# A pointwise product with 12 KB input runs, 3 KB output runs and a ring of one-supertile slots

## The chip, the cores and the metric

The kernel runs on one core of a Trainium2 chip. The metric is the device time of one execution in microseconds, the median of several runs; lower is better. Engine names are those of the profile: PE multiplies matrices, PEld is its weight load, DVE and ACT work on vectors, POOL and SP here mostly issue DMAs.

## The reference

```
out = xp[:, :H, :W, :] * dw[0, 0]          # k = 1: no padding, one product per channel
return jnp.einsum('bhwc,cd->bhwd', out, pw)
```

x is (1, 384, 384, 384), dw is (1, 1, 384) and pw is (384, 384), all bf16. So it is 147,456 rows of 384 channels, each channel scaled by dw, times a 384 x 384 matrix. Both kernels scale pw by dw once (w_r) and then compute x times w_r.

## The kernel before

**Rows and tiles.** 512 rows are a supertile, 288 in all. A chunk is one to four supertiles: 1, 1, 2, 4 at the start, then 68 chunks of four, and 4, 2, 2 at the end, 75 chunks. A chunk of x is loaded into one of four buffers X (line 143). Within each supertile, partition p gets four neighbouring rows, 3 KB in one run.

**Transposes.** PE contracts over the partitions, so channels have to lie there. DVE transposes 32 x 32 blocks of 32-bit words, a word being two neighbouring channels (line 248). There are twelve instructions for a chunk, each for one block of 64 channels and every other slot, all supertiles of the chunk at once; each writes runs of 32 neighbouring words. Their output goes to one of two buffers T, each for a whole chunk.

**Product.** For a supertile PE makes 48 matmuls (line 170): 6 channel blocks x 2 channels of a word (par) x 4 partition groups q of 32. The four groups work side by side, each into a PSUM buffer of its own; two sets of four are used in turn (PS). The set is free when ACT (s_a) and DVE (s_d) have copied it. PE's program is straight-line for the first four chunks and the last three, and between them a loop of 34 turns with eight supertiles each. PE waits for T once per chunk (lines 189 and 208).

**Copies and stores.** ACT copies q = 0, 1 and 2 of a supertile in three instructions (line 295), DVE copies q = 3 (line 289), to one of three output buffers O. DVE's program is in order: in front of each copy stand a share of the next chunk's transposes. When the chunk's last supertile is copied, POOL issues four stores (line 307), each from 32 partitions, with runs of 768 B in the output.

**Order of the queues.** SP issues all loads of x, one after the other, each as soon as the transposes of the chunk four before it are done; in front of the third it waits for pw. POOL issues all stores. At the start ACT issues dw and two loads of pw, SP the other two. dw is spread over all partitions, masked and reduced on DVE (lines 257 to 269) to give each partition its scalars (dwsel); DVE then makes the twelve pieces of w_r (line 226). The first supertile's matmuls each wait for their piece only (first_ever).

Of the kernel before, what the change touches and what calls it, by code (L numbers as in the profile page):

```python
# [10 lines left out]
ADD = mybir.AluOpType.add  # L11
MUL = mybir.AluOpType.mult

GMAX = 4
PRO = [1, 1, 2, 4]


def _plan(n_groups: int):
    if n_groups < 24:
        chunks = []  # L20
        left = n_groups
        for g in PRO:
            if left <= 0:
                break
            g = min(g, left)
            chunks.append(g)
            left -= g
        while left > 0:
            g = min(GMAX, left)
            chunks.append(g)  # L30
            left -= g
        return chunks, 0, []
    L = (n_groups - 16) // 8
    E = n_groups - 8 - 8 * L
    epi = []
    rest = E - 4
    while rest >= GMAX:
        epi.append(GMAX)
        rest -= GMAX
    if rest > 0:  # L40
        epi.append(rest)
    epi += [2, 2]
    assert sum(PRO) + 8 * L + sum(epi) == n_groups
    return list(PRO), L, epi


@with_exitstack
def kernel(
# [6 lines left out]
    NX: int = 4,  # L55
    NO: int = 3,
    pw_on_sp: int = 1,
):
    nc = tc.nc
# [5 lines left out]
    assert C == 384 and D == 384 and N % 512 == 0  # L65
    NB = C // 64
    m_max = 4 * GMAX
# [3 lines left out]

    pro, L, epi = _plan(N // 512)
    chunks = pro + [GMAX] * (2 * L) + epi
    NT = len(chunks)
    n_pro = len(pro)
    t_loop0, t_loop1 = n_pro, n_pro + 2 * L
    row0 = [0] * NT
    j0 = [0] * NT
    acc_r = acc_j = 0
    for t, g in enumerate(chunks):  # L80
        row0[t], j0[t] = acc_r, acc_j
        acc_r += 512 * g
        acc_j += g
    NST = acc_j
    if L:
        assert j0[t_loop0] % 8 == 0 and t_loop0 % 2 == 0
# [7 lines left out]
    dwb = consts.tile([P, C], BF16, name="dwb")  # L94
    ones = consts.tile([P, 4, 32], F32, name="ones")
    maskq = consts.tile([P, 4, 32], F32, name="maskq")
    mask32 = consts.tile([P, 32], F32, name="mask32")
    prod = consts.tile([P, NB * 2, 32], F32, name="prod")
    dwsel = consts.tile([P, NB * 2], F32, name="dwsel")
    warm = consts.tile([P, 1], F32, name="warm")  # L100

    Xs = [bufp.tile([P, m_max, C], BF16, name=f"X{i}") for i in range(NX)]
    Ts = [bufp.tile([P, NB, m_max, 64], BF16, name=f"T{i}") for i in range(2)]
    Os = [bufp.tile([P, m_max, D], BF16, name=f"O{i}") for i in range(NO)]
    PS = [[psum.tile([P, D], F32, name=f"ps{s}_{q}") for q in range(4)] for s in range(2)]

    s_x = [nc.alloc_semaphore(f"s_x{i}") for i in range(NX)]
    s_t = [nc.alloc_semaphore(f"s_t{i}") for i in range(2)]
    s_pe = nc.alloc_semaphore("s_pe")
    s_a = [nc.alloc_semaphore(f"s_a{i}") for i in range(8)]  # L110
    s_d = [nc.alloc_semaphore(f"s_d{i}") for i in range(8)]
# [3 lines left out]
    s_pw_sw = nc.alloc_semaphore("s_pw_sw")  # L115
    s_mask = nc.alloc_semaphore("s_mask")
    s_wr = nc.alloc_semaphore("s_wr")
    s_dv = nc.alloc_semaphore("s_dv")

    with tc.tile_critical():  # L120
        dw_row = dw.rearrange("a e c -> (a e) c")
        pw_v = pw.rearrange("(b w r) d -> w b (r d)", w=32, r=2)

        def load_pw(eng, q):
            sem = s_pw_sw if eng is nc.gpsimd else s_pw
            eng.dma_start(pw_r[32 * q : 32 * q + 32].rearrange("w b r d -> w b (r d)"), pw_v).then_inc(sem, 16)
# [4 lines left out]
        if not pw_on_sp:  # L131
            load_pw(nc.scalar, 0)
            load_pw(nc.scalar, 1)
        for t in range(NT):
            if t == 1 and pw_on_sp:
                load_pw(nc.sync, 0)
                load_pw(nc.sync, 1)
# [5 lines left out]
            d = nc.sync.dma_start(Xs[i][:, : 4 * G, :].rearrange("p (g sl) c -> p g (sl c)", sl=4), src)  # L143
            if t >= NX:
                tp = t - NX
                d._wait_ge(s_t[tp % 2], tp // 2 + 1)
            d.then_inc(s_x[i], 16)

        nc.gpsimd.memset(ones[:], 1.0).then_inc(s_mask)
        nc.gpsimd.affine_select(  # L150
            out=maskq[:],
            in_=ones[:],
            pattern=[[-32, 4], [-1, 32]],
            compare_op=mybir.AluOpType.is_equal,
            fill=0.0,
            base=0,
            channel_multiplier=1,
        )._wait_ge(s_mask, 1).then_inc(s_mask)

        nc.scalar.copy(warm[:], ones[:, 0, 0:1])._wait_ge(s_mask, 1)  # L160

        def pe_supertile(tb, g, j, wait_a=None, wait_d=None, first_ever=False):
            s = j % 2 if isinstance(j, int) else None
            for b in range(NB):
                for par in range(2):
                    for q in range(4):
                        lhsT = Ts[tb][32 * q : 32 * q + 32, b, 4 * g : 4 * g + 4, :].rearrange("p s e -> p (s e)")[
                            :, par::2
                        ]
                        mm = nc.tensor.matmul(  # L170
                            PS[s][q][:],
                            lhsT=lhsT,
                            rhs=w_r[32 * q : 32 * q + 32, b, par, :],
                            start=(b == 0 and par == 0),
                            stop=(b == NB - 1 and par == 1),
                            tile_position=(32 * q, 0),
                        )
                        if b == 0 and par == 0 and q == 0 and wait_a is not None:
                            mm._wait_ge(*wait_a)
                        elif b == 0 and par == 0 and q == 3 and wait_d is not None:  # L180
                            mm._wait_ge(*wait_d)
                        elif first_ever and q == 0:
                            mm._wait_ge(s_wr, 2 * b + par + 1)
                        if b == NB - 1 and par == 1 and q == 3:
                            mm.then_inc(s_pe)

        def pe_chunk_static(t):
            tb = t % 2
            nc.tensor.wait_ge(s_t[tb], t // 2 + 1)
            for g in range(chunks[t]):  # L190
                j = j0[t] + g
                wa = wd = None
                if j >= 2:
                    wa = (s_a[(j - 2) % 8], (j - 2) // 8 + 1)
                    wd = (s_d[(j - 2) % 8], (j - 2) // 8 + 1)
# [150 lines left out]
```

## Time and profile before

| what | value |
|---|---|
| time, median of 3 runs (lowest to highest) | 613.34 us (612.08 to 613.62) |
| profiled execution, span | 610.8 us |
| PE, PEld, DVE, ACT, POOL busy | 572.1, 422.0, 452.0, 359.4, 193.1 us |
| moved by DMA in the span, mean rate | 228.12 MB, 373 GB/s |
| queue of stores (POOL): packets, MB | 32512, 113.27 |
| queue of SP's loads: packets, MB | 38480, 113.84 |

The profile is of one execution; no time other than its span was taken of that execution itself, so its span is set beside the median of the runs, 2.5 us above it. Busy times are unions: four matmuls side by side count once. Rows of a chain or a timeline begin with start and duration in us; in the groups by line, "busy, mean ns of one" is followed by the idle time in front of them and by what ended it. "issue" means that the engine waited for nothing that the profile shows. The granted clock is a share of PE's full clock.

### The profile page before, as it was taken

To read this page: it belongs to the slowest core of one execution; us is meant where nothing else is said; L and a number is where in the kernel's file an instruction comes from. 1 tells how busy PE (TensorE), PEld (TensorE's weight loads), DVE (VectorE), ACT (ScalarE), POOL (GpSimd) and SP (SyncE) were. 2 spreads that over 40 slices of the span, in tenths; PEclk is the share of its full clock that TensorE was granted. 3 is DMA by queue.
4 is the path that set the end of the run, shared out by engine and by line. 5 is a ranking of instruction groups with operands and counts; after the bars stand their busy time and mean duration, and the time that the engine had idled before them with its cause. 6 is when DMAs were issued, how large, how long until landed. Compare 5 with 4: busy or idle time off the path is not lost.

```text
span 610.8 us, 30631 instructions
## 1 busy us (share of the span) xinstructions
PE 572.1 (94%) x13824; PEld 422.0 (69%) x13824; DVE 452.0 (74%) x1203; ACT 359.4 (59%) x866; POOL 193.1 (32%) x306
## 2 busy tenths in 40 slices
PE   1979999999999998999989999999998999999991
PEld 0546888888888665888866777766666666777771
DVE  4866778877777866877767787777875777878860
ACT  0445666666666664666655666666665556666661
POOL 0422333333333232333322333333332233333333
PEclk9999999999999998999999999999999999999997
DMA  6999999999999999999999999999999999999976
GB/s 171 407 405 385 348 382 390 397 397 387 390 381 383 396 387 379 387 398 387 383 391 401 391 396 373 384 385 393 394 393 391 383 394 386 392 396 399 359 215 182
DMA packets 71584, 228.12 MB, mean 373 GB/s; under 512 B 6081, under 2 KB 11585, under 8 KB 71553
## 3 DMA queue, kind: packets, MB, share of 16 engines
q0 software_dynamic: 32512, 113.27, 51.0%
q1 hardware_dynamic: 38480, 113.84, 48.5%
q10 hardware_dynamic: 560, 0.69, 0.5%
q8 instruction: 9, 0.15, 0.1%
q14 instruction: 23, 0.18, 0.1%
HBM read 114.52 MB, written 113.25 MB: 373 GB/s over the span
## 4 chain that ended last, share of the span: by engine, by line
PE 69%; DMA 24%; DVE 3%; issue 1%; POOL 1%; ACT 1%; SPq 0%; ACTq 0%; DVEq 0%
PE ps_0_82 L170 25%; PE ps_0_86 L170 24%; DMA X_76<-in_x_dram 11%; DMA X_74<-in_x_dram 9%; PE ps_3_85 L170 5%; PE ps_3_89 L170 5%; PE ps_1_87 L170 4%; PE ps_1_83 L170 4%; DMA out_dram<-O_79 2%; DVE T_78 L248 2%; DMA pw_r<-in_pw_dram 2%; PE ps_2_88 L170 1%; PE ps_2_84 L170 1%; POOL out_dram L307 1%; ACT O_79 L295 0%
## 5 line engine op out<-in xcount | busy, mean ns | idle before, releaser
L170 PE MATMUL ps_0_82<-w_r,T_77 32*128 32x384 bf16 x876 | 157.6, 325 | 12.6 <-DVE w_r L226 12.5
L170 PE MATMUL ps_3_85<-w_r,T_77 32*128 32x384 bf16 x876 | 157.2, 326 | 4.8 <-DVE O_80 L289 2.7
L170 PE MATMUL ps_2_84<-w_r,T_77 32*128 32x384 bf16 x876 | 157.8, 325 | 0.0
L170 PE MATMUL ps_1_83<-w_r,T_77 32*128 32x384 bf16 x876 | 157.8, 325 | 0.0
L170 PE MATMUL ps_3_89<-w_r,T_78 32*128 32x384 bf16 x864 | 153.1, 322 | 1.4 <-issue 1.4
L170 PE MATMUL ps_0_86<-w_r,T_77 32*128 32x384 bf16 x864 | 152.7, 322 | 1.6 <-issue 1.6
L170 PE MATMUL ps_3_85<-w_r,T_78 32*128 32x384 bf16 x852 | 150.0, 321 | 4.3 <-DVE O_79 L289 2.4
L170 PE MATMUL ps_1_87<-w_r,T_78 32*128 32x384 bf16 x864 | 153.1, 322 | 0.1
L170 PE MATMUL ps_0_86<-w_r,T_78 32*128 32x384 bf16 x864 | 153.1, 322 | 0.0
L170 PE MATMUL ps_2_88<-w_r,T_78 32*128 32x384 bf16 x864 | 153.1, 322 | 0.0
L170 PE MATMUL ps_2_88<-w_r,T_77 32*128 32x384 bf16 x864 | 152.7, 322 | 0.0
L170 PE MATMUL ps_1_87<-w_r,T_77 32*128 32x384 bf16 x864 | 152.7, 322 | 0.0
L170 PE MATMUL ps_3_89<-w_r,T_77 32*128 32x384 bf16 x864 | 152.5, 322 | 0.0
L170 PE MATMUL ps_0_82<-w_r,T_78 32*128 32x384 bf16 x852 | 150.5, 321 | 1.5 <-DVE T_78 L248 1.5
L170 PE MATMUL ps_2_84<-w_r,T_78 32*128 32x384 bf16 x852 | 150.7, 321 | 0.0
L170 PE MATMUL ps_1_83<-w_r,T_78 32*128 32x384 bf16 x852 | 150.7, 321 | 0.0
L170 PEld LDWEIGHTS ps_0_82<-w_r,T_77 32*128 32x128 bf16 x876 | 79.8, 94 | 47.0 <-DVE w_r L226 13.3
L307 POOL DMA_DIRECT2D out_dram<-O_79 x100 | 64.4, 650 | 148.9 <-ACT O_79 L295 147.0
L307 POOL DMA_DIRECT2D out_dram<-O_81 x100 | 64.1, 647 | 131.1 <-ACT O_81 L295 128.4
L307 POOL DMA_DIRECT2D out_dram<-O_80 x100 | 63.9, 646 | 128.4 <-ACT O_80 L295 128.4
L170 PEld LDWEIGHTS ps_0_86<-w_r,T_78 32*128 32x128 bf16 x864 | 80.3, 93 | 31.0 <-issue 2.6
L170 PEld LDWEIGHTS ps_0_82<-w_r,T_78 32*128 32x128 bf16 x852 | 77.0, 93 | 35.6 <-issue 9.7
(53 smaller groups left out, 1930.3 us busy)
## 6 DMA issues: line engine op xcount, KB each, us to landing
out_dram<-O_79 POOLq DMA_DIRECT2D x96, 384.0 KB, 9.5
out_dram<-O_80 POOLq DMA_DIRECT2D x92, 384.0 KB, 9.5
out_dram<-O_81 POOLq DMA_DIRECT2D x92, 384.0 KB, 9.5
X_76<-in_x_dram SPq DMA_DIRECT2D x18, 1536.0 KB, 23.6
X_73<-in_x_dram SPq DMA_DIRECT2D x18, 1536.0 KB, 24.1
X_74<-in_x_dram SPq DMA_DIRECT2D x17, 1536.0 KB, 23.9
X_75<-in_x_dram SPq DMA_DIRECT2D x17, 1536.0 KB, 24.7
X_75<-in_x_dram SPq DMA_DIRECT2D x2, 768.0 KB, 10.7
```

What stands on the lines that cost most here:

```text
L170: mm = nc.tensor.matmul(PS[s][q][:], lhsT=lhsT, rhs=w_r[32 * q : 32 * q + 32, b, par, :], start=(b == 0 and par == 0), stop=(b == NB - 1 a ...
L248: ins = nc.vector.transpose(out=Tw[:, b, h:mm_:2, :], in_=Xw[:, h:mm_:2, 32 * b : 32 * b + 32])
L307: sd = nc.gpsimd.dma_start(dstv[sl], Os[o][32 * sl : 32 * sl + 32, : 4 * G, :])
```

## The change

- A chunk is now mapped in one piece: partition p gets 4L neighbouring rows of a chunk of L supertiles (12 KB in one run for L = 4). Supertile j of the chunk takes the rows k L + j of each partition, k = 0 to 3. The output row of group q, PSUM partition m = 4 i + k, is then q 128 L + m L + j, so a store has runs of L rows (3 KB for L = 4) on all 128 partitions.
- To put the rows in that order, a transpose writes its 32 words with a step of four words ("p b (i k) -> p b k i"). There are two transposes for a supertile, each of three channel blocks (384 words per partition), with a semaphore of its own.
- T holds one supertile per slot, two slots. DVE's order is: copy of jj, transposes of jj + 2, which wait for PE's half of jj.
- PE is a loop of 144 turns with two supertiles each. It waits for all twelve w_r before the loop, and for each half of T. s_pe counts half supertiles.
- ACT copies q = 0 to 2 in one instruction; PS is one PSUM tile of four 2 KB rows per set.
- SP issues loads and stores, one store per chunk; there are four buffers O. POOL issues no DMA.
- dw is loaded by 32 partitions in pieces of two channels and copied to the four groups on DVE; w_r is made half by DVE and half by ACT. The loads of x no longer wait for pw.
- Chunks: 1, 1, 2, then 70 of four, then 2, 1, 1.

```diff
-        nc.scalar.dma_start(dwb[:], dw_row.to_broadcast((P, C))).then_inc(s_dw, 16)
...
-            if t == 2:
-                nc.sync.wait_ge(s_pw, 16 * 4)
-            i = t % NX
-            G = chunks[t]
-            src = xf[row0[t] : row0[t] + 512 * G, :].rearrange("(g p sl) c -> p g (sl c)", p=P, sl=4)
...
+        def load_x(t):
+            L = chunks[t]
+            r = 512 * s0[t]
+            src = xf[r : r + 512 * L, :].rearrange("(p s) c -> p (s c)", p=P)
+            d = nc.sync.dma_start(Xs[t % NX][:, : 4 * L, :].rearrange("p s c -> p (s c)"), src)
+            if t >= NX:
+                je = s0[t - NX] + chunks[t - NX] - 1
+                d._wait_ge(s_t[je % 2][1], je // 2 + 1)
+            d.then_inc(s_x[t % NX], 16)
+
+        def store(t):
...
+            nc.sync.wait_ge(s_d[je % 2], je // 2 + 2)
+            dst = of[r : r + 512 * L, :].rearrange("(q p j) d -> p q (j d)", q=4, p=P)
+            d = nc.sync.dma_start(dst, Os[t % NO][:, : 4 * L * D].rearrange("p (q e) -> p q e", q=4))
+            d._wait_ge(s_a[je % 2], je // 2 + 2)
+            d.then_inc(s_o[t % NO], 16)
...
+        nc.scalar.dma_start(dwt[:], dw_v).then_inc(s_dw, 16)
+        load_x(0)
+        load_pw(nc.scalar, 2)
+        load_pw(nc.sync, 0)
+        load_pw(nc.scalar, 3)
+        load_pw(nc.sync, 1)
+        for t in range(1, NX):
+            load_x(t)
         for t in range(NT):
...
+            if t + NX < NT:
+                load_x(t + NX)
+            store(t)
...
+        def supertile(s, rv):
             for b in range(NB):
                 for par in range(2):
                     for q in range(4):
...
+                        if par == 0 and q == 0 and b in (0, 3):
+                            nc.tensor.wait_ge(s_t[s][b // 3], rv)
                         mm = nc.tensor.matmul(
...
+                            lhsT=Ts[s][32 * q : 32 * q + 32, b, par::2],
...
+                        if b in (2, 5) and par == 1 and q == 3:
                             mm.then_inc(s_pe)
...
+        nc.tensor.wait_ge(s_wr, 2 * NB)
+        with nc.tensor.Fori(0, NS // 2, 1) as it:
+            rv = nc.tensor.to_reg(it + 1)
+            for s in range(2):
+                supertile(s, rv)
...
+        def transposes(t, j):
...
+            Xw = Xs[t % NX][:].bitcast(U32)[:, : 4 * L, :].rearrange("p (k l) c -> p k l c", l=L)
+            Tw = Ts[s][:].bitcast(U32).rearrange("p b (i k) -> p b k i", k=4)
+            for h in range(2):
...
+                ins = nc.vector.transpose(
+                    out=Tw[:, 3 * h : 3 * h + 3],
+                    in_=Xw[:, :, j, 96 * h : 96 * h + 96].rearrange("p k (b w) -> p b k w", w=32),
+                )
+                if jj >= 2:
+                    ins._wait_ge(s_pe, 2 * (jj - 2) + h + 1)
+                ins.then_inc(s_t[s][h])
...
+        transposes(*order[0])
+        for b in range(NB):
+            for r in range(2):
+                eng = nc.vector if r == 0 else nc.scalar
...
+                if r == 0:
+                    i = nc.vector.tensor_scalar_mul(w_r[:, b, r, :], pw_r[:, b, r, :], sc)
+                else:
+                    i = nc.scalar.activation(w_r[:, b, r, :], pw_r[:, b, r, :], COPY, scale=sc)
...
+            e = nc.vector.tensor_copy(Ov[:, 3, j, :], PS[s][:, 3, :D])
+            e._wait_ge(s_pe, 2 * jj + 2)
+            e.then_inc(s_d[s])
+            a = nc.scalar.copy(Ov[:, 0:3, j, :], PS[s][:, 0:3, :D])
+            a._wait_ge(s_pe, 2 * jj + 2)
+            a.then_inc(s_a[s])
+            if jj + 2 < NS:
+                transposes(*order[jj + 2])
```

More of the change, by code (lines that the diff above doesn't have):

```diff
@@ L10, with _chunks @@
 U32 = mybir.dt.uint32
[L11 to L44, printed above, removed]
+COPY = mybir.ActivationFunctionType.Copy
+LMAX = 4
+NX = 4
+NO = 4
+def _chunks(n_super: int):
+    head, tail = [1, 1, 2], [2, 1, 1]
+    mid = n_super - sum(head) - sum(tail)
+    assert mid > 0 and mid % LMAX == 0
+    return head + [LMAX] * (mid // LMAX) + tail
 @with_exitstack
@@ L149 @@
[L149 to L163, printed above, removed]
+            if t + NX < NT:
+                load_x(t + NX)
@@ L187, in pe_chunk_static @@
[L187 to L195, printed above, removed]
-                pe_supertile(tb, g, j, wa, wd, first_ever=(j == 0))
-        for t in range(0, t_loop0 if L else NT):
-            pe_chunk_static(t)
```

231 lines of the change are left out of this document (60 added, 171 removed).

## The prediction

> **What bounds the kernel now.** I read the sums by stage first, then the queues, then the chain of waits.
>
> ```profile
> 340.00:458.00 118.00, 118.00 (x2911) 80.05 (x2904) 92.85 (x242) 75.41 (x183) 38.76 (x60) 1.00 1.03 389
> 12.00:20.00 8.00, 7.50 (x108) 3.51 (x112) 7.63 (x38) 1.59 (x4) 1.90 (x4) 1.00 0.87 315
> 20.00:60.00 40.00, 33.79 (x812) 23.12 (x808) 28.00 (x74) 20.79 (x51) 12.71 (x21) 1.00 1.03 399
> 228.00:240.00 12.00, 9.74 (x203) 5.60 (x195) 6.18 (x17) 4.97 (x12) 2.59 (x4) 0.86 1.03 385
> 310.00:340.00 30.00, 27.66 (x656) 18.33 (x652) 20.91 (x56) 16.58 (x41) 10.35 (x16) 1.00 1.03 395
> 458.00:515.00 57.00, 54.09 (x1284) 35.94 (x1280) 40.36 (x108) 32.78 (x80) 16.49 (x26) 1.00 1.03 391
> ```
>
> Each row is a stretch: its length, then busy time and count of PE, weight loads, DVE, ACT and POOL, the granted clock, the DMA share and GB/s. In an undisturbed stretch PE makes 2911 matmuls in 118 us, 40.5 ns each; 48 of them are a supertile of 512 rows, 1.95 us. The same period stands between two copies of a PSUM buffer:
>
> ```profile
> 419.64 0.56 DVE L289 CAST O_79<-ps_3_85 128x384 bf16<-128x384 f32 x1 [0.39 <-PE ps_3_85 L170]
> 420.12 1.09 DVE L248 STREAM_TRANSPOSE T_77<-X_73 128x256 uint32<-128x256 uint32 x3
> 421.59 0.56 DVE L289 CAST O_79<-ps_3_89 128x384 bf16<-128x384 f32 x1 [0.39 <-PE ps_3_89 L170]
> ```
>
> 288 supertiles x 1.95 us = 561.6 us is what PE cannot go below with these matmuls, and the change keeps all 13824. PE begins at 12.46 us and ends at 598.5 us:
>
> ```profile
> 12.09 2.84 DVE L226 TENSOR_SCALAR w_r<-pw_r,dwsel 128x384 bf16<-128x384 bf16 x12 [1.58 <-DMA pw_r<-in_pw_dram]
> 12.46 0.50 PE L170 MATMUL ps_0_82<-w_r,T_77 32*128 32x384 bf16 x1 [12.46 <-DVE w_r L226]
> 598.18 0.32 PE L170 MATMUL ps_3_89<-w_r,T_77 32*128 32x384 bf16 x1
> ```
>
> That is 586.0 us, 24.4 more than the work. By the stretches (length less count x 40.5 ns): about 3 us before 20 us, 7 from 20 to 60, 3.8 at 228, 3.4 at 310, 5.0 at 458. The chain of waits names what ended them:
>
> ```profile
> 12.45 7.94 DMA X_76<-in_x_dram
> 37.29 1.64 issue
> 44.31 1.62 issue
> 51.31 1.36 issue
> 202.70 28.34 DMA X_74<-in_x_dram
> 300.55 29.24 DMA X_74<-in_x_dram
> 444.63 28.93 DMA X_76<-in_x_dram
> ```
>
> The three holes of the middle follow loads that took 28 to 29 us; the same 1.5 MB took 7.94 us at the start. So the loads fall behind. A supertile reads and writes 2 x 512 x 384 x 2 B = 786 kB, and in 1.95 us that is 403 GB/s; the DMA moves 389 with a busy share of 1.03. **PE and DMA are bounds within 4% of each other**: PE sets the pace, and now and then the loads take it over. The three "issue" pieces, 4.6 us, are PE waiting for nothing but its own instructions, all in the first 52 us.
>
> **The change part by part.**
>
> *PE.* Same matmuls, same tiles: 561.6 us. The straight-line pieces before and after the loop go, so I drop the 4.6 us. In their place come two waits per supertile (one per half of T), 576 in all, and 144 turns of the loop for 34. What a wait and a turn cost on PE:
>
> ```profile
> PEld ps_0_82 L170 <- issue: 16.5, 72, 2.0
> PE ps_0_86 L170 <- issue: 1.6, 1, 1.6
> ```
>
> At the 75 chunk starts now (wait, and in 34 of them the loop's turn) a weight load comes 0.23 us late on average, 16.5 us in 72 times, yet the matmuls' own "issue" waits are only the three pieces above: the lead of the weight loads covers it. I cost it at nothing; without that cover it is a rival below.
>
> *Start.* The first matmul now waits for all twelve w_r, not for the first. After the pw loads land (12.09 us) ACT makes six of them; an ACT copy of 384 takes 0.37 us from start to start (below), so 6 x 0.37 = 2.2 us beside DVE's six. PE begins at 12.09 + 2.4 = 14.5 us, 2.0 later. X1 to X3 are issued right behind pw on SP, with no wait for pw: pw may land some us later or the same; DVE's w_r and PE's start wait behind it. dw now comes as 192 pieces of 4 B and stands ahead of two pw loads on ACT's queue and of DVE's first transposes; four small copies replace the product and the reductions. All of that lies before pw lands, unless dw takes over 10 us (it takes 5.8 now). Bounds 12.5 to 18 us, I keep 14.5. The slow first matmuls (108 in 8 us) stay, 3 us.
>
> *ACT.* One copy of 3 x 384 for three of 384:
>
> ```profile
> 419.64 0.48 ACT L295 CAST O_79<-ps_0_82 128x384 bf16<-128x384 f32 x1 [0.71 <-PE ps_3_85 L170]
> 420.02 0.48 ACT L295 CAST O_79<-ps_1_83 128x384 bf16<-128x384 f32 x1
> 420.39 0.50 ACT L295 CAST O_79<-ps_2_84 128x384 bf16<-128x384 f32 x1
> ```
>
> 1.25 us of 1.95 now, no more afterwards: nothing, hidden beside PE.
>
> *DVE.* This decides. Per supertile: the copy, and two transposes of 384 words for three of 256. The same 768 words; but the output view "p b (i k) -> p b k i" with k=4 makes each write step 16 B on, where before 32 neighbouring words were written. In a stretch where DVE waits for nothing:
>
> ```profile
> 475.20 1.00 DVE T_78 L248 x3
> 476.20 0.44 DVE O_80 L289
> 476.64 1.00 DVE T_78 L248 x3
> ```
>
> ```profile
> L248 DVE STREAM_TRANSPOSE T_78<-X_76 128x256 uint32<-128x256 uint32 x216 | 78.0, 413 | 11.4 <-DMA X_76<-in_x_dram 9.8 <-PE ps_3_85 L170 1.5
> L248 DVE STREAM_TRANSPOSE T_78<-X_74 128x64 uint32<-128x64 uint32 x12 | 1.6, 206 | 0.0
> L269 DVE TENSOR_REDUCE dwsel<-prod 128x12 f32<-128x384 f32 x1 | 0.6, 553 | 0.0
> L257 DVE TENSOR_REDUCE mask_69<-maskq 128x32 f32<-128x128 f32 x1 | 0.4, 369 | 1.7 <-POOL maskq L150 1.7
> ```
>
> A transpose of 256 follows the next after 0.334 us; 256 and 64 words differ by 207 ns, about 1.05 ns a word, which leaves 67 ns fixed. At that rate DVE would need 0.44 + 2 x (384 x 1.05 + 67) = 1.38 us of 1.95. No row writes in 16 B steps. The nearest reads in wide steps: the reduction at L257 goes through its 128 words in steps of 128 B and takes 369 ns; the one at L269, contiguous, takes 553 for 384, so 153 ns beside 384 x 1.04. (369 - 153) / 128 = 1.69 ns a word. Bounds: 1.05, and 2.88 if all of the 369 went on its words. I take 1.69, the only row with wide steps: 0.44 + 2 x (649 + 67) = 1.87 us. **PE still ends last, by 0.08 us of 1.95.** The point of change is 1.79 ns a word.
>
> The Trainium skill speaks against this edit. "Vector Engine (DVE) Microarchitecture Reference", section "Measured stream behaviour on trn2", says that a port keeps its full rate only while elements come in runs of at least two adjacent words, and gives, for a destination moved at every element, 1.71 ns a column for 4 KiB hops and 2.50 for steps of 24 words. The row at L257 agrees with the first; no run here shows the second. By the first the sum stays what it is, by the second DVE takes 2.49 us and the time would be an estimated 748 us.
>
> The ring of two slots of one supertile: the transposes of jj+2 stand on DVE behind the copy of jj, which waits for PE. From PE's end of jj, 0.48 + 0.72 us to the first half and 0.72 more to the second, 1.92 us: PE starts jj+2 after 1.95 and needs the second half 0.97 later. Nothing, as long as DVE's sum is below PE's; above it PE waits for T each time.
>
> *DMA.* Loads take 12 KB runs for 3 KB, stores 3 KB runs for 768 B, on all partitions in one issue of SP (0.40 us by the first row) for four of POOL (2.32 us). POOL has nothing else to do afterwards; SP issues 152 times, 61 us of the span.
>
> ```profile
> 12.01 0.40 SPq L143
> ...
> 600.09 2.32 POOL L307 DMA_DIRECT2D out_dram<-O_81  x4 [1.75 <-ACT O_81 L295]
> ```
>
> ```profile
> 16.00:18.00 2.00, 1.96 (x28) 0.76 (x24) 1.93 (x10) 1.24 (x3) 0.00 (x0) 1.00 1.03 416
> 18.00:20.00 2.00, 2.00 (x44) 1.04 (x40) 1.79 (x9) 0.35 (x1) 1.90 (x4) 1.00 1.03 409
> out_dram<-O_81 POOLq DMA_DIRECT2D x8, 192.0 KB, 5.8
> ...
> dwb<-in_dw_dram ACTq DMA_DIRECT2D x1, 96.0 KB, 5.8
> ```
>
> Before the first stores the loads alone ran at 409 to 416; half loads, half stores run at 389. So stores alone move at 1 / (2/389 - 1/409) = 371 GB/s. Afterwards the store has the run length that the load has now: between 371 (nothing gained: 389 mixed) and 409 mixed; I take 409, above the 403 that PE asks. Below nothing: one queue that alternates load and store could be poorer than two; the mean over the whole span, 373, bounds that.
>
> On SP the order is load t+4, store t, load t+5. The store waits for both copies of its last supertile, some 1.3 us after the chunk's end, and load t+5 stands behind it; that load's own buffer comes free only about 4 us later, so nothing is late. At the start store 0 holds load 5 back to about 20 us; chunk 5 is wanted at about 36.
>
> *End.* PE ends at 14.5 + 3 + 561.6 = 579.1. The copy of the last supertile takes 1.2 us, one issue on SP 0.4, 384 KB land in about 5 us (192 KB took 5.8 in four pieces; 1.5 MB took 7.94). The last issue of before began at about 601.8 and landed 5.8 later, 607.6, and the span ended 3.2 us behind it; I keep 3. Sum: 579.1 + 9.6 = 588.7 us of span. The median of the runs, 613.34, lies 2.5 over the span of the profiled execution, 610.8; with that, **591 us**. Of the 22 us gained, some 14 are late loads with what followed them, 4.6 PE's instructions, 2.7 the shorter end, the rest small holes before 60 us; 2 are lost at the start.
>
> **The rivals.**
>
> *DVE becomes the bound (slower).* For it: the wide write steps, and a margin of only 0.08 us. Against it: 1.69 from the one row with wide steps. It decides from 1.79 ns a word; level with before is (613.3 - 29.6) / 288 = 2.03 us per supertile, 1.89 ns a word. At twice the contiguous rate, 2.1 ns, DVE takes 2.19 us: 288 x 2.19 + 29.6 = 660 us (29.6 being 591.2 less 561.6). At the bound of 2.88 with no fixed part, 2.65 us and 793.
>
> *The runs are longer and the DMA no faster.* The busy share is 1.03 already, and it may hang on bytes alone. At 389 a chunk of 3.15 MB takes 8.09 us against PE's 7.80; 71 chunks fall back 20.5 us. A load is issued three chunks, 23.4 us, before its first transposes and takes 8 alone, so some 15 us can build up before PE waits; 6 us of waiting and 2 of slowed clock (0.86 at 228) make 599. At 373 it would be 8.43 us a chunk, 45 - 15 = 30 us of waiting, 621. The Trainium skill's "DMA: Bandwidth & Descriptors", section "Issuing engines are not separate DMA queues", holds that another issuing engine saves issue time only; on the move to SP alone, this rival is what it says. No run shows it yet.
>
> *PE pays for its waits.* If 0.07 us of each late weight load (0.23 less one round of 0.16) showed at 576 waits, that is 40 us: 631. Against it: none shows now.
>
> **How the numbers follow.** Forecast, PE the bound: 0.52, its own range 584 to 602. DVE the bound: 0.33, of which half lies above 680. DMA no faster: 0.10. PE's waits: 0.05. The range that leaves out about 2 in 10 reaches to 680. Below 584 PE would have to start no later than now and the end to shrink more. A difference of 0.3% is about what a measurement of this kernel can tell from none. Faster: 0.52 + 0.10 + 0.01 of DVE just above its point; the same 0.03 from there; slower 0.34.
>
> **What would show it.** Right: transposes with a mean below 0.82 us (at 1.79 ns a word 384 words take 0.83: 413 ns less 256 x 1.05 leaves 144), matmuls without idle time between 60 and 570 us, DMA near 403 GB/s, load landing times that don't grow, PE's first matmul near 14.5. Wrong: transposes well over 0.83 us and PE waiting for T in each supertile (DVE); landing times that grow to 25 us and more (DMA); "issue" before matmuls (PE's waits).

## The result, and the profile after

The changed kernel takes **588.14 us** (median of 4 runs, 587.01 to 588.73); before took 613.48 us in the same comparison (4 runs, 612.08 to 614.41). The ratio is 0.9587, its 95% interval 0.9567 to 0.9607. The forecast was 591 us, with 584 to 602 as the range of its likeliest case. The span of the profiled execution is 586.0 us, 24.8 under that of before. In two of the kernels below, experiments 6 and 8, one run of four took 1563 and 1949 us, in a slow state that the other three don't show; their times are medians of those three.

First the same stretches as in the prediction, now of after (length, busy time and count of PE, PEld, DVE, ACT, POOL, granted clock, DMA share, GB/s):

```profile
340.00:458.00 118.00, 118.00 (x2912) 80.13 (x2907) 118.00 (x183) 67.49 (x61) 0.00 (x0) 1.00 1.02 404
...
228.00:240.00 12.00, 12.00 (x304) 8.14 (x300) 12.00 (x20) 7.01 (x7) 0.00 (x0) 1.00 1.01 389
...
458.00:515.00 57.00, 57.00 (x1412) 38.71 (x1404) 57.00 (x89) 32.89 (x30) 0.00 (x0) 1.00 1.02 401
```

The count of matmuls in the undisturbed stretch is what it was, 2912 in 118 us. The two stretches that had holes before are full, and the slowed clock at 228 us (0.86) is gone. DVE is recorded as busy for all of it, which looks like a second bound; the experiments show that it isn't one. The chain of waits of after (start, duration, what) says the same in its longest pieces:

```profile
1.88 7.55 DMA pw_r<-in_pw_dram
...
9.52 3.15 ACT w_r L199 x6
...
13.00 547.95 PE ps L134 x13435
...
562.11 14.82 DMA out_dram<-O
...
577.01 1.12 ACT O L215
```

PE stands in the chain from 13.0 us to 561 us; no load of x stands in it any more. The piece at 562 us is a store whose buffer the last supertile's copy needs. It costs little: PE itself has no hole, and ACT starts that copy about half a microsecond late. Last, rows from the page of after: busy time by engine, two groups of DVE (busy, mean ns of one, idle before), and the DMA issues (KB each, median us to landing):

```profile
PE 563.5 (96%) x13824; PEld 382.1 (65%) x13824; DVE 564.0 (96%) x876; ACT 326.8 (56%) x297; POOL 0.3 (0%) x5
...
L174 DVE STREAM_TRANSPOSE T<-X 128x384 uint32<-128x384 uint32 x576 | 448.7, 858 | 0.0
L212 DVE CAST O<-ps 128x384 bf16<-128x384 f32 x288 | 160.4, 557 | 6.3 <-PE ps L134 4.5
...
X<-in_x_dram SPq DMA_DIRECT2D x70, 1536.0 KB, 14.1
out_dram<-O SPq DMA_DIRECT2D x70, 1536.0 KB, 15.7
```

Where the 24.8 us of span came from: PE took 586.0 us from its first matmul to its last and now takes 563.5 (22.5 less); what follows PE took 12.3 us and now takes 586.0 - 13.0 - 563.5 = 9.5 (2.8 less); PE starts 0.5 later. So the whole gain is in PE's holes and the end, as forecast. What the result alone doesn't tell is which part of the change closed the holes: longer loads, longer stores, one queue, or the other order of work.

### The profile page after: what moved, and what is told of

Same layout as the page of the kernel before. It is cut to its first block, busy times and chain, and to the rows that moved or that the text cites. A ratio compares the mean times of both kernels' runs of the same rounds, so it can differ in the third digit from the quotient of the medians.

```text
span 586.0 us, 30055 instructions
## 1 busy us (share of the span) xinstructions
PE 563.5 (96%) x13824; PEld 382.1 (65%) x13824; DVE 564.0 (96%) x876; ACT 326.8 (56%) x297; POOL 0.3 (0%) x5
## 4 chain that ended last, share of the span: by engine, by line
PE 94%; DMA 4%; ACT 1%; SPq 0%; issue 0%; ACTq 0%
PE ps L134 94%; DMA out_dram<-O 3%; DMA pw_r<-in_pw_dram 1%; ACT w_r L199 1%; ACT O L215 0%; SPq L89 0%; SPq L95 0%; SPq L245 0%; ACTq L211 0%; ACTq L194 0%; SPq L84 0%
## 5 line engine op out<-in xcount | busy, mean ns | idle before, releaser
L134 PE MATMUL ps<-w_r,T 32*128 32x384 bf16 x13824 | 563.5, 322 | 13.0 <-ACT w_r L199 13.0
L134 PEld LDWEIGHTS ps<-w_r,T 32*128 32x128 bf16 x13824 | 382.1, 93 | 194.0 <-issue 13.0
L215 ACT CAST O<-ps 128x1152 bf16<-128x1152 f32 x288 | 322.1, 1118 | 243.3 <-PE ps L134 242.1
L174 DVE STREAM_TRANSPOSE T<-X 128x384 uint32<-128x384 uint32 x576 | 448.7, 858 | 0.0
L212 DVE CAST O<-ps 128x384 bf16<-128x384 f32 x288 | 160.4, 557 | 6.3 <-PE ps L134 4.5
L199 ACT ACTIVATE w_r<-pw_r,dwsel 128x384 bf16<-128x384 bf16 x6 | 3.1, 602 | 5.6 <-DMA pw_r<-in_pw_dram 5.6
L197 DVE TENSOR_SCALAR w_r<-pw_r,dwsel 128x384 bf16<-128x384 bf16 x6 | 1.5, 316 | 2.4 <-DMA pw_r<-in_pw_dram 2.4
```

What stands on the lines that cost most here:

```text
L134: mm = nc.tensor.matmul(PS[s][:, q, :D], lhsT=Ts[s][32 * q : 32 * q + 32, b, par::2], rhs=w_r[32 * q : 32 * q + 32, b, par, :], start=(b = ...
L174: ins = nc.vector.transpose(out=Tw[:, 3 * h : 3 * h + 3], in_=Xw[:, :, j, 96 * h : 96 * h + 96].rearrange("p k (b w) -> p b k w", w=32),)
L197: i = nc.vector.tensor_scalar_mul(w_r[:, b, r, :], pw_r[:, b, r, :], sc)
L199: i = nc.scalar.activation(w_r[:, b, r, :], pw_r[:, b, r, :], COPY, scale=sc)
L212: e = nc.vector.tensor_copy(Ov[:, 3, j, :], PS[s][:, 3, :D])
L215: a = nc.scalar.copy(Ov[:, 0:3, j, :], PS[s][:, 0:3, :D])
```

## The experiments

Each kernel below is after with one edit, unless it says otherwise; the name in brackets is the one that the expectations use, and the diffs show the main lines. Ratios are against before on the same chip, with their 95% intervals; before took 609.8 to 614.8 us there. After's own ratio of 0.9587 is the one to compare with.

**1. Both runs short, one queue (e1_short_runs).** The old mapping of rows comes back for loads and stores, all else stays, so SP issues stores with 768 B runs.

```diff
-            src = xf[r : r + 512 * L, :].rearrange("(p s) c -> p (s c)", p=P)
+            src = xf[r : r + 512 * L, :].rearrange("(g p sl) c -> p g (sl c)", p=P, sl=4)
...
-            dst = of[r : r + 512 * L, :].rearrange("(q p j) d -> p q (j d)", q=4, p=P)
+            dst = of[r : r + 512 * L, :].rearrange("(g p) d -> p g d", p=P)
```

> The changed kernel with the row mapping of before: loads in 3 KB runs, stores in 768 B runs, all else as changed. Theory A (the longer runs make each byte cheaper for the DMA): the DMA falls back faster than the 0.17 us a chunk of the changed kernel, load landing times pass 25 us before the end, PE waits some 5 to 15 us, 593 to 603 us. Theory B (one queue that alternates loads and stores is enough, the run length does little): 586 to 590 us with landing times as now.

Measured: 695.52 us, ratio 1.1358 (1.1272 to 1.1443), far outside what was expected. From the page and the waits of this kernel (waits: us in total, times, longest):

```profile
q1 hardware_dynamic: 187168, 227.09, 100.2%
```

```profile
PE ps L134 <- DVE T L174: 93.6, 115, 2.8
```

PE now waits 93.6 us for T, which waits for X. The reason is in the packets. Before moved its 768 B runs in a queue of POOL's, 32512 packets for 113 MB, most of 4608 B: six runs in one. SP's queue makes one packet of each run, 187168 in all. So this kernel isn't "after without its long runs"; it has something that neither kernel had. What it shows, with experiment 2 beside it, is that the stores can go to SP without loss only together with their longer runs.

**2. Loads alone short (e1b_load3k).** The stores stay as in after; a chunk's load becomes four issues with runs of 3 KB.

```diff
-            src = xf[r : r + 512 * L, :].rearrange("(p s) c -> p (s c)", p=P)
-            d = nc.sync.dma_start(Xs[t % NX][:, : 4 * L, :].rearrange("p s c -> p (s c)"), src)
+            src = xf[r : r + 512 * L, :].rearrange("(p k l) c -> k p (l c)", p=P, k=4)
+            for k in range(4):
+                d = nc.sync.dma_start(Xs[t % NX][:, k * L : k * L + L, :].rearrange("p s c -> p (s c)"), src[k])
```

> Loads alone back to 3 KB runs (four issues per chunk, same rows to the same places), stores keep 3 KB runs. Theory A: packets of 3 KB take 121 to 127 ns against 460 to 504 for 12 KB in the two traces, about 3% more DMA time for half of the bytes; landing times grow faster, 588 to 592 us. Theory B: 588 us. If the loads' runs carry the whole gain, it comes near the first experiment.

Measured: 603.23 us, ratio 0.9857 (0.9787 to 0.9926): 15 us of after's gain are gone, more than either theory had. The stretch after 300 us, and ACT's waits:

```profile
300.00:570.00 270.00, 264.49 (x6389) 186.31 (x6381) 254.78 (x399) 148.98 (x134) 0.00 (x0) 1.00 1.02 384
```

```profile
ACT O L216 <- DMA out_dram<-O: 48.0, 32, 4.0
```

384 GB/s at a share of 1.02, less than the 403 that PE asks. Here the wait shows on the stores' side: ACT can't copy because O isn't free. In this kernel each issue of a load also takes SP 0.88 us at the median, against 0.33 in after, so the 15 us may hold something of the five issues per chunk in one queue; experiment 5 puts the stores into another.

**3. Stores issued by POOL (e2_pool_store).** The runs stay as in after; only the issuing engine changes back.

```diff
-            nc.sync.wait_ge(s_d[je % 2], je // 2 + 2)
+            nc.gpsimd.wait_ge(s_d[je % 2], je // 2 + 2)
...
-            d = nc.sync.dma_start(dst, Os[t % NO][:, : 4 * L * D].rearrange("p (q e) -> p q e", q=4))
+            d = nc.gpsimd.dma_start(dst, Os[t % NO][:, : 4 * L * D].rearrange("p (q e) -> p q e", q=4))
```

> Stores issued by POOL, one per chunk as now, same runs; loads stay on SP. Theory A: the bytes cost the same, so 586 to 592 us. Theory B (order of the one queue): loads fall behind while stores land early, as before; landing times of loads grow to 25 us and more, PE waits, 595 to 605 us.

Measured: 586.69 us, ratio 0.9588 (0.952 to 0.9655), the same as after. With 3 KB runs no difference in time can be told between the two issuing engines. But the landing times split; the issues of this kernel:

```profile
X<-in_x_dram SPq DMA_DIRECT2D x70, 1536.0 KB, 9.9
out_dram<-O POOLq DMA_DIRECT2D x70, 1536.0 KB, 15.5
```

In after both grew over the span, loads from 8.2 us (issue at 28.7) to 20.3 (at 527.9). Here loads stay near 10 us to the end, and only stores grow, from 13 to 22.

**4. Stores short, in POOL's queue (e10_store768_pool).** 12 KB loads, stores with 768 B runs issued by POOL, one issue for a chunk.

```diff
-            dst = of[r : r + 512 * L, :].rearrange("(q p j) d -> p q (j d)", q=4, p=P)
-            d = nc.sync.dma_start(dst, Os[t % NO][:, : 4 * L * D].rearrange("p (q e) -> p q e", q=4))
+            dst = of[r : r + 512 * L, :].rearrange("(q p j) d -> p j q d", q=4, p=P)
+            d = nc.gpsimd.dma_start(dst, Os[t % NO][:, : 4 * L * D].rearrange("p (j q d) -> p j q d", q=4, d=D))
```

> The loads of after, in 12 KB runs, with the stores as before the change: 768 B runs, issued by GpSimd, one issue for a chunk. Engine time for a MB was 40.7 us with 12 KB loads and 3 KB stores, and 44.0 for the 768 B stores of before. If the run length of the stores is a term of its own, the mean is 42.4 us a MB, 389 GB/s at the busy share of 1.03 that two queues reached, less than the 403 that PE asks: holes in PE that follow loads, DMA share at 1.02 or more, time 600 to 612 us. If the loads' run length alone was what mattered, no holes, 586 to 589 us.

Measured: 588.22 us, ratio 0.9583 (0.9543 to 0.9622), after's time. The issues, and two pieces of the chain:

```profile
X<-in_x_dram SPq DMA_DIRECT2D x70, 1536.0 KB, 10.2
out_dram<-O POOLq DMA_DIRECT2D x70, 1536.0 KB, 21.8
```

```profile
507.67 26.01 DMA out_dram<-O
...
535.25 43.11 PE ps L135 x948
```

The loads are as quick as in experiment 3. The stores take 22 us and at 507.67 even 26.01; there PE loses 2.1 us, once, because O wasn't free. Beside experiment 3 the span is 1.7 us longer (586.6 and 584.9) and the median 1.5, and the ratios, 0.9583 and 0.9588, don't tell the two apart. So the stores' short runs cost 2 us at most in POOL's queue, not the 12 to 24 that would follow from the stores' 44.0 us per MB of before. Before issued them in four DMAs of 32 partitions each; that difference is not tested.

**5. Loads short, stores by POOL (e11_load3k_pool).** Experiments 2 and 3 together.

> The loads of e1b_load3k, four of 3 KB runs for a chunk, with the stores in 3 KB runs issued by GpSimd. Theory A, the loads' run length costs capacity whatever the queue, and where packets of two queues meet, the queue with the smaller packets falls behind: the loads (3072 B against 6144 B) land later and later, up to 20 us and more, the stores stay near 10, PE waits for T behind X, and the time is 598 to 612 us, like e1b_load3k or worse. With 12 KB loads it was the other way round: loads flat at 10, stores growing to 22. Theory B, who falls behind does not depend on packet size: loads stay at 10 us, stores grow, ACT waits for O, 598 to 606 us. Theory C, e1b_load3k lost its time to five issues in one queue of SyncE, not to the run length: 585 to 590 us, no waits.

Measured: 596.88 us, ratio 0.9721 (0.9683 to 0.976): 10 us above experiment 3, with the loads' run length as the only difference but for the four issues, which no run separates from it. The number lies just under theory A's range; its signs are all there. The stretch, the chain, the stores' landing time, DVE's waits:

```profile
300.00:570.00 270.00, 263.58 (x6444) 191.59 (x6439) 258.86 (x403) 149.96 (x134) 25.18 (x34) 1.00 1.00 387
```

```profile
281.84 23.45 DMA X<-in_x_dram
...
523.84 23.42 DMA X<-in_x_dram
```

```profile
out_dram<-O POOLq DMA_DIRECT2D x70, 1536.0 KB, 10.6
```

```profile
DVE T L175 <- DMA X<-in_x_dram: 13.4, 13, 3.6
```

With 3 KB loads the loads fall behind and the stores stay at 10.6 us; with 12 KB loads it was the other way round. Late loads stand in the chain again, as in before, but what is late differs: here, by its counts, a single DMA engine, in before about half of them (the table of counts in the next section).

From its first matmul to its last PE takes 573.6 us here, 564.2 in experiment 3 and 586.0 in before. So shorter loads bring back 9.3 of the 21.8 us between before and experiment 3. Another 4.6 are the three pieces of "issue"; the other 8 no experiment isolates.

The five together, as engine time per MB (the time that all packets of a queue took between 100 and 500 us, over their bytes), and the time of the kernel:

```
kernel                     loads            stores           mean    GB/s   us
before                     41.0 (3072 B)    43.5 (4608 B)    42.3    389    613.5
1 both short, SP           50.0 (3072 and 768 B, one queue)  50.0    323    695.5
2 loads short, SP          42.0 (3072 B, one queue)          42.0    388    603.2
5 loads short, POOL        43.5 (3072 B)    38.5 (6144 B)    41.0    396    596.9
4 stores short, POOL       39.4 (12288 B)   41.7 (4608 B)    40.6    402    588.2
after, SP                  40.4 (12288 and 3072 B)           40.4    403    588.1
3 after, stores by POOL    41.5 (12288 B)   38.5 (6144 B)    40.0    404    586.7
```

Sizes are those of most packets. PE's 403 GB/s at the busy share of 1.02 leave 16 x 1.02 / 403 GB/s = 40.5 us per MB. The kernels near that are bound by PE, those above it by the DMA (experiments 2 and 5 by its latest engine, as the counts in the next section show), and the order of the means is the order of the times in all seven, though before's time also holds its start and its longer end. Where PE sets the pace a packet's time can hold some waiting, so these numbers rank and don't measure a capacity.

**6. A long loop (e3_long_loop).** Eight supertiles in a turn, 36 turns for 144.

```diff
-        with nc.tensor.Fori(0, NS // 2, 1) as it:
-            rv = nc.tensor.to_reg(it + 1)
-            for s in range(2):
-                supertile(s, rv)
+        with nc.tensor.Fori(0, NS // 2, 4) as it:
+            for u in range(4):
+                rv = nc.tensor.to_reg(it + (u + 1))
+                for s in range(2):
+                    supertile(s, rv)
```

> PE's loop with eight supertiles in 36 turns for two in 144. If the short loop took away the three pieces of 'issue' in the first 52 us (4.6 us), they come back in the first turn: 590 to 594 us, with holes of 1.4 to 1.6 us before 30 us. If those pieces came from the straight-line code ahead of the loop, 588 us. If PE paid for the turns of the short loop, it gets faster than 588.

Measured: 588.66 us, ratio 0.9616 (0.9518 to 0.9715), a span of 586.8 us, no "issue" in front of a matmul after the first. The length of the loop is worth nothing that can be told, and the three "issue" pieces of before don't come back.

The trace of before shows where they lay: in front of matmuls 476, 603 and 731 (counted from 0). The straight-line code holds the first 384, so all three lay in the first turn of the loop. Each began within 0.2 us of the end of a 16 KB packet of the queue that the page of before lists as "instruction" (q8; these packets end at 37.4, 44.5 and 51.3 us). That PE waited there for its own program is argued from this. Experiment 6 has such packets at 27.5 and 32.8 us and no hole, so what makes the wait stays open.

**7. Transposes that write without steps (e4_contig_t).** The columns of T stand in the order (k, i) for (i, k), so the output's rows come out in another order within groups of 128.

```diff
-            Tw = Ts[s][:].bitcast(U32).rearrange("p b (i k) -> p b k i", k=4)
+            Tw = Ts[s][:].bitcast(U32).rearrange("p b (k i) -> p b k i", k=4)
```

> The transposes write runs of 32 neighbouring words; nothing else is changed, so the rows of each group of 128 come out in another order. The step from transpose to transpose measures the price of the 16 B steps: with 1.05 ns a word 0.47 us, against 0.71 in the changed kernel. PE the bound: time stays at 586 to 589. If DVE were the bound in the changed kernel, or its late second half held PE back, the time falls by more than 3 us.

Measured: 587.70 us, ratio 0.9563 (0.9528 to 0.9597), no change. The group of transposes, and two rows of the timeline (start, duration); below them the same rows of after, with the copy that comes next:

```profile
L174 DVE STREAM_TRANSPOSE T<-X 128x384 uint32<-128x384 uint32 x576 | 295.4, 551 | 2.3 <-DMA X<-in_x_dram 2.2
```

```profile
420.45 0.56 DVE L212 CAST O<-ps 128x384 bf16<-128x384 f32 x1 [0.45 <-PE ps L134]
420.93 1.03 DVE L174 STREAM_TRANSPOSE T<-X 128x384 uint32<-128x384 uint32 x2
```

```profile
420.57 0.56 DVE L212 CAST O<-ps 128x384 bf16<-128x384 f32 x1
421.05 1.56 DVE L174 STREAM_TRANSPOSE T<-X 128x384 uint32<-128x384 uint32 x2
...
422.52 0.56 DVE L212 CAST O<-ps 128x384 bf16<-128x384 f32 x1
```

Two transposes are one row here. 1.56 us less the 0.85 of the second is 0.71 us from the start of the first to the start of the second; 0.71 less the 0.067 of the prediction is 1.67 ns a word over 384. Without steps the second takes 0.53, so the step is 1.03 - 0.53 = 0.50 us, 1.1 ns a word. At PE's pace these steps can hold some waiting; in experiment 8, where DVE sets the pace, two transposes take 1.37 us, 0.69 each, which is 1.61 ns a word. So a stepped write costs about 0.2 us a transpose, 0.4 us of each 1.95, and DVE had that to spare. The second row of after also shows how the 100% of DVE is to be read: the pair ends at 422.61 by its record, 0.09 us behind the start of the next copy. Records overlap at their ends, and 100% is no proof of a bound.

**8. DVE a little slower (e5_dve_more).** One more transpose of 64 words for each supertile, behind the copy, on data of its own.

```diff
             e.then_inc(s_d[s])
+            x5 = nc.vector.transpose(out=idle_b[:].bitcast(U32), in_=idle_a[:].bitcast(U32))
+            x5._wait_ge(s_ds, 5 + jj)
+            x5.then_inc(s_ds)
```

> One more DVE instruction per supertile, a transpose of 64 words (0.207 us alone, 0.13 from start to start). DVE's sum in the changed kernel is 0.48 + 2 x 0.71 to 0.73, a margin of 0.01 to 0.05 us of 1.95. So 0.08 to 0.12 us show at each of 288 supertiles: 611 to 623 us, and PE waits for T. If DVE has a wider margin that the records hide: 588.

Measured: 589.28 us, ratio 0.9591 (0.9546 to 0.9636), far under the 611 to 623 that the records had let expect. The timeline and PE's waits:

```profile
420.88 0.54 DVE L215 CAST O<-ps 128x384 bf16<-128x384 f32 x1
421.34 0.20 DVE L218 STREAM_TRANSPOSE idle_b<-idle_a 128x64 uint32<-128x64 uint32 x1
421.47 1.52 DVE L177 STREAM_TRANSPOSE T<-X 128x384 uint32<-128x384 uint32 x2
...
422.84 0.54 DVE L215 CAST O<-ps 128x384 bf16<-128x384 f32 x1
```

```profile
PEld ps L136 <- issue: 66.9, 281, 13.1
```

From copy to copy it is now 1.96 us, made of 0.46 for the copy, 0.13 for the added transpose and 1.37 for the two others. PE's 1.95 is just exceeded: weight loads come late 281 times, and PE takes 568.8 us for 563.5. So DVE's own sum in after is 1.96 - 0.13 = 1.83 us, a margin of 0.12, where 0.01 to 0.05 had been expected from the records. PE ends 5.4 us later than in after (581.9 and 576.5), the span only 1.5: the last of the 16 counts of the last store comes 0.4 us behind the 15th, where in after it is 3.9. So some 4 us of after's end are a wait for one DMA engine, and the time by itself hides that PE was held up.

**9. DVE relieved (e6_act_all).** ACT copies all four quarters, DVE only transposes.

```diff
-            e = nc.vector.tensor_copy(Ov[:, 3, j, :], PS[s][:, 3, :D])
-            e._wait_ge(s_pe, 2 * jj + 2)
-            e.then_inc(s_d[s])
-            a = nc.scalar.copy(Ov[:, 0:3, j, :], PS[s][:, 0:3, :D])
+            a = nc.scalar.copy(Ov[:, :, j, :], PS[s][:, :, :D])
```

> ACT copies all four PSUM rows in one instruction (about 1.45 us of 1.95), DVE only transposes (about 1.45). PE the bound: 586 to 589 us, DVE idle a quarter of the time. If PE's first matmuls then wait for ACT (copy ends 1.45 us after PE's end, 0.5 before it is needed): over 590.

Measured: 586.91 us, ratio 0.9547 (0.9512 to 0.9583); the interval overlaps with after's. The group:

```profile
L169 DVE STREAM_TRANSPOSE T<-X 128x384 uint32<-128x384 uint32 x576 | 504.9, 877 | 60.3 <-PE ps L133 4.7
```

DVE has 60 us of idle time now, and no gain in time can be told. Experiments 7 to 9 settle it: DVE isn't the bound, but 0.13 us more in each supertile makes it one by a hair.

**10. The start (e7_start).** The first turn of PE's loop is written out, and each of its matmuls waits only for its own piece of w_r.

```diff
+                        if first and q == 0:
+                            nc.tensor.wait_ge((s_wr, s_wa)[par], b + 1)
...
-        nc.tensor.wait_ge(s_wr, 2 * NB)
-        with nc.tensor.Fori(0, NS // 2, 1) as it:
+        supertile(0, 1, first=True)
+        supertile(1, 1)
+        with nc.tensor.Fori(1, NS // 2, 1) as it:
```

> The first turn of PE's loop is written out, and its first supertile waits for each piece of w_r alone. PE begins at about 9.9 us for 13.0. If PE's start sets the end: 585 us. If the slowest DMA engine sets it (in the changed kernel 15 of 16 counts of the last store are there at 580.7 us, the last at 584.6): 587 to 588 us, and its lag at the end grows by what PE gains.

Measured: 585.53 us, ratio 0.9531 (0.9492 to 0.957). From the chain:

```profile
9.88 547.92 PE ps L137 x13440
...
558.97 15.95 DMA out_dram<-O
```

PE starts at 9.88 in place of 13.0. Of those 3.1 us the span keeps 2.0 (584.0). At 571.4 us PE stands for 0.5 us, because the transposes wait 0.8 us for the last load of x: 15 of its 16 counts were there at 560.5, the last came at 570.8. And the store of 558.97 is behind as in after: the last supertile's copy begins at 575.0, 0.9 us after PE's end.

**11 and 12. Versions for speed (e8_both, e9_start_pool).** Experiment 10 with the copies of 9, and experiment 10 with the stores of 3.

> The start of e7_start and the copies all on ACT, as in e6_act_all; stores still from SyncE. If PE is the bound and the end hangs on one DMA engine that is behind with the stores, the ACT copies change nothing and the time is that of e7_start, 584 to 587 us, with PE starting near 10 and ending near 574, and the last store's last count some 8 us behind PE's end. If DVE's copies were still costing PE something, it comes below 583.

> The start of e7_start, and the stores issued by GpSimd, as in e2_pool_store. There the last store landed 5 us behind the last copy instead of 8. If the slow DMA engine's backlog sits in the queue that loads and stores share, PE starts near 10, runs without a hole to 573, the last store lands by 579 and the time is 583 to 585 us, 1 to 2 under e8_both. If the backlog follows the engine whatever the queue, the time is e8_both's within 0.5 us.

Measured: 583.86 us, ratio 0.9511 (0.9481 to 0.954), and **583.17 us**, ratio 0.9501 (0.9472 to 0.953). Both intervals lie below that of after, by 0.8 to 0.9% at the middle, so these two beat both kernels. Between themselves they overlap, so whether POOL's queue shortens the whole isn't settled by the times. The chain of the second:

```profile
9.61 0.33 DVE w_r L201
...
10.08 563.81 PE ps L138 x13183
...
573.92 1.13 ACT O L219
...
575.33 0.75 POOL out_dram L108
```

The last store lands 3.2 us after its issue, at 578.5, in place of 6.5 in after; POOL's drain then takes 1.7 of that back. PE starts 3 us earlier than in after; what is left beside PE's 563.8 us is 10.1 us ahead of it and 7.4 behind.

## Why the prediction was right

**PE's sum: right.** 561.6 us of work and 3 us for slow first matmuls were forecast; 563.5 was measured, so the slow start costs 1.9.

**The straight-line pieces: the term right, its ground wrong.** 4.6 us were dropped and didn't come back, with a short loop or a long one. But they were dropped because the straight-line code goes, and the pieces lay in the first turn of the loop (experiment 6). Why they are gone isn't shown, so this term came out right partly by luck.

**PE's waits at nothing: right.** 576 waits and 144 turns show as no wait of PE or of its weight loads after the first 13.0 us; these are all the rows of the two (us in total, times, longest):

```profile
PE ps L134 <- ACT w_r L199: 13.0, 1, 13.0
PEld ps L134 <- issue: 13.0, 1, 13.0
```

The rival of 631 us falls.

**The start: sum off by 1.5 us, both terms wrong.** 14.5 was forecast, 13.0 measured. pw landed at 9.43, not at 12.09, though X1 to X3 follow it on SP at once. The six pieces of w_r took 3.15 us on ACT, 0.525 each, not 0.37: the copies from which 0.37 was taken are another operation on another form.

**DVE: right, and by a margin of the size forecast.** 1.69 ns a word was taken from one reduction that reads in wide steps; 1.61 to 1.67 came out for a transpose that writes in steps. The sum was 1.87 us, by experiment 8 it is 1.83. That two so different instructions cost nearly the same is luck as far as these runs show. The price without steps was read a little low: 207 ns over 192 words is 1.08 ns, not 1.05, and leaves 58 ns fixed for 67; the sum hardly feels it. The Trainium skill's "Vector Engine (DVE) Microarchitecture Reference", section "Measured stream behaviour on trn2", gives 1.71 ns for a destination that hops at every element and 2.50 for steps of 24 words; the 1.61 to 1.67 of a step of four words in this transpose is near the first, and the 748 us of the second didn't come. One sign was badly chosen: "a mean below 0.82 us is right, well over 0.83 is wrong". The mean is 0.858, yet a transpose follows the other after 0.71. The recorded duration holds a tail beside which the next instruction runs, 0.15 us here and 0.08 in before's transposes (0.413 recorded, 0.334 from start to start); the step from start to start was the thing to name.

**DMA: the verdict right, the step behind it wrong, so by luck.** The prediction took the 389 GB/s of before apart as "loads alone 409, so stores alone 371", gave the whole gain to the stores' runs and nothing to the loads'. The runs say the opposite. Stores of 768 B in POOL's queue, beside 12 KB loads, cost 2 us at most (experiment 4); loads of 3 KB cost 10 us with the stores on POOL and 15 with them on SP (experiments 5 and 2). The flaw is that 409 to 416 was the rate of loads that had the DMA engines nearly to themselves (the row of 409 already holds the first four store issues); what loads and stores cost in a mix can't be told from it. The 409 for the mix was never put to the test: after moves 401 and 404 in the two long stretches shown, what PE asks, and how much more it could do is open.

**Who falls behind.** Experiments 3, 4 and 5 and after itself agree with one rule: where two queues meet, the one with smaller packets falls behind. 3072 B against 6144 B: the loads, on one engine. 12288 B against 4608 or 6144 B: the stores. All in one queue: both alike. The Trainium skill's "DMA: Bandwidth & Descriptors", section "Queues, rings and completion order", says that a DMA engine takes turns between the queues for which it has work, a packet at a time; that fits, if its packets are those that the records list. In before it was 3072 B of loads against 4608 B of stores, and it was the loads that took 28 us, the stores 9.5. That this is the cause there too is argued from the same sizes; before itself wasn't run with other packets.

**"Landing times that don't grow": wrong.** They grew in after from 8 to 20 us while PE never waited. Each DMA is split over 16 engines and reports 16 counts; the times at which they came, read from the trace:

```
                              issued
after, a load:                504.5  first 510.5, 8th 512.7, 15th 514.8, 16th 523.6
after, a store:               538.7  first 547.2, 8th 548.4, 15th 551.1, 16th 560.4
3 (stores by POOL), a load:   505.5  first 511.5, 8th 512.9, 15th 515.3, 16th 515.5
3 (stores by POOL), a store:  540.0  first 546.3, 8th 546.6, 15th 551.1, 16th 557.9
2 (loads short, SP), a store:  501.8  first 508.9, 8th 509.2, 15th 510.3, 16th 518.6
5 (loads short), four issues: 521.7  first 525.5, 60th of 64 532.8, then 541.8, 544.3, 545.2, 547.3
4 (stores short), a store:    507.7  first 518.4, 8th 521.9, 15th 529.7, 16th 533.7
before, a load of the chain:  444.6  first 455.3, 8th 464.9, 15th 473.4, 16th 473.6
```

In after, in experiment 2 and in the stores of experiment 3 fifteen counts come within 1 to 5 us, and the last 7 to 9 us behind them. In experiment 5 it is the last four, one for each issue. By the counts, one engine of the sixteen falls behind over the span; whether it is slower or has more to do they don't say. The load of experiment 5 and the store of experiment 2 stand in the chains of these kernels: what PE waits for there is in the end one engine. In before it wasn't one engine: the counts of that load are spread over 18 us, and nine of them come more than 20 us after the issue. So after isn't only bound by PE; it is within reach of its latest DMA engine. Loads are issued some 23 us ahead, and at 20 us that was nearly used up when the kernel ended. A kernel with many more rows would probably have met it; experiment 10 did, in its last load. Experiment 4 waited once for a store of 26 us, but there several counts came late.

**The end: right in sum, not in its terms.** 9.6 was forecast, 9.5 measured; two errors cancel, which is luck. The last store took 6.5 us for 5: its 15th count came at 580.8, its 16th at 584.6. The close took 1.4 for 3, since POOL has no DMA to drain: its drain takes 0.04 us here; where POOL issues the stores it takes 0.4 in experiment 4, 1.7 in experiment 3 and 2.35 in before.

**The rivals.** DVE as the bound falls, though by only 0.12 us of 1.95. "The runs are longer and the DMA no faster" falls for the loads' runs; for the stores' runs, and for the move to SP by itself, it is nearly what happened. The Trainium skill's rule on issuing engines ("DMA: Bandwidth & Descriptors", section "Issuing engines are not separate DMA queues") agrees with the times of experiment 3 and after, which are alike. It stops at 768 B runs: in POOL's queue they cost 588.2 - 586.7 = 1.5 us (experiments 4 and 3), which isn't clear of none, in SP's 695.5 - 603.2 = 92 us (experiments 1 and 2).

## What to carry to other kernels

Look at the run length of loads and stores apart, and at the packets that each queue makes of them: 768 B runs were nearly harmless in a queue that packs six of them and cost 92 us in one that doesn't. A mean rate and a mean busy share hide the latest of 16 DMA engines; landing times that grow steadily while nobody waits are the sign that the margin is being used up. And judge an engine by an instruction added to it, or by the step from start to start, which is an upper bound where the engine may be waiting: both 96% of PE and 96% of DVE stood on the page of after, and only one of them was the bound.

## What the runs showed of the hardware that was not expected

SP's queue makes one packet of each run (768 B: 36 ns median; 3072 B: 121; 12288 B: 460), POOL's packs runs (six of 768 B into 4608 B, 184 to 191 ns; two of 3072 B into 6144 B, 234). One DMA engine of 16 lags behind the others by up to 10 us in after, which has no queue of POOL's, and by up to 14 in experiment 12, which has one; in before and in experiment 4 the late counts are several. Which engine it is, and whether it is the same in every run, the records don't say. Per byte a 12288 B packet takes at the median 5% less than a 3072 B one (37.4 and 39.4 ns for 1000 B). That would be enough for the 4% by which experiment 2 lies above after in engine time per MB, but under load the means of the two (502 and 122 ns in after) don't show it, so why longer loads are cheaper stays open.
